# Pooled attention and two MLPs: keys by head into other rooms, looks behind attention, and the second MLP's tiles prepared one tile earlier

## The chip, the cores and the metric

One Trainium2 chip, one of its cores. The metric is the device time of one execution in microseconds (us). The kernel before takes 1679.4 us (median of three runs, 1678.56 to 1681.44).

## The reference

```python
k_p = k.reshape(B, H, Sp, pool, D).mean(axis=3)
v_p = v.reshape(B, H, Sp, pool, D).mean(axis=3)
scores = scale * np.matmul(q, k_p.transpose(0, 1, 3, 2))
scores = scores - np.max(scores, axis=-1, keepdims=True)
attn = np.exp(scores)
attn = attn / (np.sum(attn, axis=-1, keepdims=True) + 1e-09)
x = np.matmul(attn, v_p)
...
h = x @ w_in
g = np.where(h >= 1, h, np.where(h <= -1, 0.0, (h + 1) ** 2 / 4))
y = g @ w_out
...
h = y @ w2_in
g = h * (1.0 / (1.0 + np.exp(-h)))
return (g @ w2_out).astype(np.float32)
```

There are 8 batches of 8 heads, 576 positions and 64 features; keys and values are averaged over groups of 8 positions, so 72 remain of each. The result, 4608 tokens of 512 features, goes through two MLPs with 2048 hidden features. The weights come in 64 bits, and are read as pairs of 32-bit words.

## The kernel before, in words

**Precision.** A matrix product is made of three half-precision products: each operand is split into a high and a low half (`split`: ScalarE writes the high one, L354, VectorE the low one, L355), and L120, L121 and L122 multiply high by high, low by high and high by low. A "look" finds the largest absolute value of a tile, from which its power-of-two scale is made; a small TensorE product into a tile named `all` (L107, or L247 for the first weight) carries that maximum to all partitions.

**Stages.** (1) Attention for the first four tiles of 128 tokens, in single precision: keys and values of batch 0 are loaded by pairs of heads (L397 `kv_load`, four rooms of the pool `kvp` named `raw`); the keys are summed over groups of 8 on VectorE (L420), the values on TensorE by products with a unit matrix (L413). Then come transposes of the queries (L496), scores (L526), softmax on VectorE and ScalarE (L535 to L559, L540), transposes of the weights (L574), the product with the values (L614), and the split into `xh` and `xl` (L621). (2) The first weight, 8 MB, in nine pieces `wa_128` to `wa_136`: `load1`, `look1` (ScalarE L239 takes absolute values, VectorE L240 the maximum), `scales1` (L247, L250), and `convert1`, which assembles a 32-bit word on VectorE (L95 shift, L259, L262), scales and rounds it on ScalarE (L265, L267) and takes the low half on GpSimd (L268). (3) The first MLP: nine tiles of 512 tokens, each of 16 chunks; a chunk is a group of products `hps` (`emit_h`), the activation (`pre_A`, `min_A`, `mid_A`, `post_A`, with the split at L819 and L820), and, three chunks later (`LAG`), its share of the products `y` (`emit_yA`). `evac_yA` (L839) scales a finished tile into a room of the pool `big`, which has one room, and stores it to DRAM. The rest of the attention and the conversion of the other three weights run between the chunks. (4) The second MLP: 18 tiles of 256 tokens. `tile_B(t)` (L859) prepares one in six steps: load into the room of `big` (`yin`, L865), look (L111, then `all` L107), sums on GpSimd, and three splits. `group_B(t, q, ys)` (L893) makes the hidden features in two halves, q = 0 and 1; each has seven products `hb` of 24 matmuls (a scheme with seven instead of eight products), and between these it takes the seven output products `y` of the half before it out of the list `ys` (12 matmuls each). `evac_yB` (L977, adds at L986) reads the seven finished `y` banks of a tile into the rooms `ob` and stores them; it stands after the first half of the next tile.

**What sets the order.** The Python code is the program order of a scheduler that simulates the engines and lets an instruction that is ready go ahead of one that isn't; `paced` ties work to the time at which a named step (`late[...]`) is done. Rooms are reused when their last reader has finished.

**What the main loops say.** The second MLP asks for the next tile's first three steps ahead of the first half and for its splits ahead of the second:

```python
for t in range(NTB):
    for q in range(2):
        if t + 1 < NTB:
            if q == 0:
                pend.extend(tile_B(t + 1))
            for _ in range(3):
                pend.pop(0)()
        ys = group_B(t, q, ys)
        if q == 0 and t:
            evac_yB(t - 1)
```

Of the kernel before, what the change touches and what calls it, by code (L numbers as in the profile page):

```python
# [9 lines left out]
F32 = mybir.dt.float32  # L10
# [23 lines left out]
def tile_pooled_attention_two_mlps(  # L34
# [22 lines left out]
    POOL = 8  # L57
# [295 lines left out]
    def split(hi, lo, x, s):  # L353
        a = nc.scalar.activation(out=hi, in_=x, func=AF.Copy, scale=s)  # L354
        return a, nc.vector.scalar_tensor_tensor(out=lo, in0=x, scalar=s, in1=hi, op0=ALU.mult, op1=ALU.subtract)  # L355
# [37 lines left out]

    def kv_load(b, which, hp):

        r = kv_raw[b, which, hp] = kvp.tile([SP, 2, POOL, D], F32, tag="raw", name="raw")
        src = (k if which == "k" else v)[b, 2 * hp:2 * hp + 2]  # L397
        nc.sync.dma_start(out=r, in_=src.rearrange("h (p r) d -> p h r d", r=POOL))

    def kv_pool(b, which, hp):  # L400

        if hp == 0:
            sums[b, which] = kvp.tile([SPT, H, D], F32, tag="sum", name="sum", bufs=3)
            if which == "k":
                nc.gpsimd.memset(sums[b, which][SP // 32 * 32:SPT], 0.0)
        dst = sums[b, which][0:SP, 2 * hp:2 * hp + 2]
        r = kv_raw.pop((b, which, hp))
        if (b, which) in ON_PE:
            if hp == 0:
                kv_ps[b, which] = att_ps([SP, H, D])  # L410
            ps = kv_ps[b, which]
            for n in range(POOL):
                nc.tensor.matmul(  # L413
                    out=ps[:, 2 * hp:2 * hp + 2], lhsT=ident[0:SP, 0:SP], rhs=r[:, :, n], start=n == 0,
                    stop=n == POOL - 1,
                )
            if hp == NP - 1:
                nc.scalar.copy(out=sums[b, which][0:SP], in_=kv_ps.pop((b, which)))
        else:
            nc.vector.tensor_reduce(out=dst, in_=r.rearrange("p h r d -> p h d r"), axis=AX.X, op=ALU.add)  # L420
# [62 lines left out]
    q_t, qT_t, cq_t, at_t, aT_t, kT = {}, {}, {}, {}, {}, {}  # L483

    def load_q(i):
        q_t[i] = qp.tile([128, H, D], F32, tag="q", name="qt")
        for o, n, b, s in segs(i):
            nc.sync.dma_start(out=q_t[i][o:o + n], in_=q[b, :, s:s + n, :].rearrange("h p d -> p h d"))

# [109 lines left out]
    def att_pv(i):  # L599
# [21 lines left out]
        hi, lo = (x[:, :, j * 128:(j + 1) * 128] for x in r["x"])  # L621
        for o, n, b, _ in segs(i):
            c = b - t * N // S
            split(hi[:, :, o:o + n], lo[:, :, o:o + n], ps[:, :, o:o + n], r["sv"][:, c:c + 1])
        if j == 0 and t:
            consts_A(r)

# [211 lines left out]
    def evac_yA(t):  # L839
        r = XT.pop(t)  # L840
        cy = sm.tile([128, KD], F32, tag="cy", name="cy")
        ts(cy, e2, r["ge"], 2.0 ** -29, ALU.mult, ALU.mult)
        y = big.tile([128, KD, N], F32, tag="big", name="y32")
        for d, ps in enumerate(acc_t.pop(t)):
            if d % 2:
                ts(y[:, d], ps, cy[:, d:d + 1])
            else:
                nc.scalar.activation(out=y[:, d], in_=ps, func=AF.Copy, scale=cy[:, d:d + 1])
            nc.sync.dma_start(out=ydram[t][:, d], in_=y[:, d])


    TB = 256
# [4 lines left out]
    def tile_B(t):  # L857
# [18 lines left out]
        def sums_():  # L876
            b = held["b"]
            comb_b([held["z"][:, n] for n in range(4)], b[:, 0, 0], b[:, 0, 1], b[:, 1, 0], b[:, 1, 1])
            r["x"] = [x.rearrange("p c n -> p (c n)")[:, 0:7 * 256].rearrange("p (n c f) -> p n c f", n=7, c=2)
                      for x in new_x()]  # L880

        def part(a, b, x):
            hi, lo = (y[:, a:b] if b > a + 1 else y[:, a] for y in r["x"])
            split(hi, lo, x(), r["s"])

# [3 lines left out]
    def group_B(t, q, ys):  # L889
# [36 lines left out]
        add(c11, u, product(1, 1))  # L926
        act(c11)
        halves_of(0, c11)
        y(1)
        add(u, u, product(2, 5))  # L930
        y(1)
        add(v, u, product(3, 6))
# [21 lines left out]
        minus(z4, c21, z2)  # L954
        halves_of(1, c21)
        halves_of(2, z4)
        y(1)
        if q == 0:
            r["acc"] = [ps_y.tile([128, 2, 256], F32, tag=f"y{k_}", name=f"y{k_}") for k_ in range(4)]

# [97 lines left out]

    load_to(4)
    q_to(3)  # L1060
    load1(0)
    load_to(8)
    q_to(4)
    for p in range(1, len(cuts1)):
        load1(p)
    load_to(12)
    pool_to(4)
# [9 lines left out]
    r = XT[0]  # L1077
    for a, b in ((0, 3), (3, 7), (7, 9)):
        for p in range(a, b):
            look1(p)  # L1080
        scales1(a, b)
        if a == 0:
            convert1(0)
# [16 lines left out]
    for s in range(KF + 2):  # L1100
        if s < KF:
            while n1 < min(len(cuts1), piece_of(cuts1, s) + 2):
                convert1(n1)
                n1 += 1
            emit_h(s, chunk1, r["x"])
        z = s - 1
# [44 lines left out]
    for s in range(KF, LAST + LAG):  # L1151
# [30 lines left out]
                nc.sync.dma_start(out=w4[i], in_=d4[:, i])  # L1182
        if T == NTILE - 1 and m == 3:
            pend.extend(tile_B(0))
        if pend:
            pend.pop(0)()
        z = s - LAG
# [3 lines left out]
                evac_yA(z // KF)  # L1191

    wctx.close()
    b2 = bctx.enter_context(tc.tile_pool(name="b2", bufs=1, side="right", reuse_waits="tile"))
    for i in range(4, PIECES):
        w4.append(b2.tile([128, 2, 7, 256], F16, name=f"wd{i}"))
# [3 lines left out]
    ys = []  # L1200
    for t in range(NTB):
        for q in range(2):
            if t + 1 < NTB:
                if q == 0:
                    pend.extend(tile_B(t + 1))
                for _ in range(3):
                    pend.pop(0)()
            ys = group_B(t, q, ys)
            if q == 0 and t:
                evac_yB(t - 1)  # L1210
    for f in ys:
        f()
    evac_yB(NTB - 1)
# [31 lines left out]
```

## Time and profile before

| | |
|---|---|
| median of three runs | 1679.4 us (1678.56 to 1681.44) |
| the profiled execution, its own time | 1683.29 us |
| its span | 1681.4 us |
| mean granted TensorE clock | 0.965 of full speed |
| DMA traffic | 166.35 MB, mean 99 GB/s |
| TensorE busy | 93% of the span |
| VectorE busy | 75% of the span |
| ScalarE busy | 53% of the span |
| GpSimd busy | 32% of the span |

The span runs from the first to the last recorded instruction; 1.9 us of the execution's own time lie around it. A row of the timeline gives start, duration, engine, line, operation, and behind it in brackets how long the engine had been idle and what ended that. Lines are those of the kernel before unless it is said otherwise; in the changed kernel L413 is L426, L614 is L630, L820 is L836, L910 is L934, L986 is L1010, and L239 to L355 stay.

### The profile page before, as it was taken

To read this page: it belongs to the slowest core of one execution; us is meant where nothing else is said; L and a number is where in the kernel's file an instruction comes from. 1 tells how busy PE (TensorE), PEld (TensorE's weight loads), DVE (VectorE), ACT (ScalarE), POOL (GpSimd) and SP (SyncE) were. 2 spreads that over 40 slices of the span, in tenths; PEclk is the share of its full clock that TensorE was granted. 3 is DMA by queue.
4 is the path that set the end of the run, shared out by engine and by line. 5 is a ranking of instruction groups with operands and counts; after the bars stand their busy time and mean duration, and the time that the engine had idled before them with its cause. 6 is when DMAs were issued, how large, how long until landed. Compare 5 with 4: busy or idle time off the path is not lost.

```text
span 1681.4 us, 34695 instructions
## 1 busy us (share of the span) xinstructions
PE 1561.3 (93%) x14406; PEld 1078.8 (64%) x14406; DVE 1255.0 (75%) x2204; ACT 894.9 (53%) x1420; POOL 534.7 (32%) x479
## 2 busy tenths in 40 slices
PE   6894799898999999999999979999999999999998
PEld 6542344344444444444444459999999999999998
DVE  7798887978889787897656338777766777777765
ACT  3577354666747547576655435455444454444543
POOL 1322402332424303333422023443333343334322
PEclk7897899899999999999999989999999999999999
DMA  9435587655646576353454030000100001000000
GB/s 278 129 99 140 140 218 174 145 129 137 166 118 161 141 218 167 98 131 86 133 220 148 0 138 27 27 27 27 37 30 27 27 27 39 27 27 27 27 14 27
DMA packets 217037, 166.35 MB, mean 99 GB/s; under 512 B 153904, under 2 KB 176432, under 8 KB 216880
## 3 DMA queue, kind: packets, MB, share of 16 engines
q1 hardware_dynamic: 216880, 164.14, 35.1%
q8 instruction: 113, 1.85, 0.5%
q14 instruction: 44, 0.36, 0.1%
HBM read 102.76 MB, written 33.55 MB: 81 GB/s over the span
## 4 chain that ended last, share of the span: by engine, by line
PE 31%; DVE 26%; issue 15%; ACT 10%; DMA 8%; POOL 8%; SPq 1%; DVEq 0%; POOLq 0%; ACTq 0%
DMA yin<-y 4%; PE y L120 4%; PE y L122 4%; PE y L121 4%; POOL c L681 4%; DVE sum L420 4%; DVE g L355 4%; PE hps L122 4%; PE hps L121 4%; PE hps L120 4%; DVE g L791 3%; POOL c L684 2%; DVE xl L355 2%; DVE g L820 2%; ACT g L354 2%
## 5 line engine op out<-in xcount | busy, mean ns | idle before, releaser
L121 PE MATMUL hb<-xl,wc 128*128 128x128 f16 x2016 | 349.7, 219 | 0.0
L120 PE MATMUL hb<-xh,wc 128*128 128x128 f16 x2016 | 349.7, 219 | 0.0
L122 PE MATMUL hb<-xh,wc 128*128 128x128 f16 x2016 | 349.7, 219 | 0.0
L355 DVE SCALAR_TENSOR_TENSOR g<-c,tsg,g 128x512 f16<-128x512 f32 x252 | 226.6, 902 | 87.8 <-ACT g L354 87.8
L973 PE MATMUL y<-wd,g 128*128 128x256 f16 x1008 | 274.7, 273 | 14.4 <-DVE ob L986 13.0
L975 PE MATMUL y<-wd,g 128*128 128x256 f16 x1008 | 274.8, 273 | 1.0 <-DVE g L355 0.9
L974 PE MATMUL y<-wd,g 128*128 128x256 f16 x1008 | 274.7, 273 | 0.0
L913 ACT ACTIVATE c<-c,tc 128x512 f32<-128x512 f32 x144 | 103.0, 717 | 258.8 <-DVE c L910 258.8
L120 PE MATMUL y<-g,wb 128*128 128x512 f16 x544 | 207.7, 388 | 17.3 <-ACT wb L212 15.0
L120 PE MATMUL hps<-xh,wa 128*128 128x512 f16 x576 | 221.0, 384 | 1.3 <-ACT g L780 0.9
L354 ACT ACTIVATE g<-c,tsg 128x512 f16<-128x512 f32 x252 | 177.6, 718 | 83.7 <-POOL c L684 51.3
L121 PE MATMUL hps<-xl,wa 128*128 128x512 f16 x576 | 220.9, 383 | 0.3 <-DVE skv L95 0.3
L122 PE MATMUL hps<-xh,wa 128*128 128x512 f16 x576 | 220.6, 384 | 0.0
L910 DVE TENSOR_TENSOR c<-c,hb 128x512 f32<-128x512 f32 x252 | 167.7, 680 | 70.4 <-PE hb L122 70.1
L121 PE MATMUL y<-g,wb 128*128 128x512 f16 x544 | 211.2, 388 | 5.8 <-DVE g L820 5.8
L122 PE MATMUL y<-g,wb 128*128 128x512 f16 x544 | 210.5, 387 | 4.1 <-POOL wb L213 3.9
L121 PEld LDWEIGHTS <-wc 128*128 128x128 f16 x2016 | 197.7, 98 | 2.6
L120 PEld LDWEIGHTS <-wc 128*128 128x128 f16 x2016 | 197.7, 98 | 2.1
L122 PEld LDWEIGHTS <-wc 128*128 128x128 f16 x2016 | 197.7, 98 | 0.2
L791 DVE SCALAR_TENSOR_TENSOR g<-g,tbr,u 128x512 f32<-128x512 f32 x144 | 127.4, 886 | 59.2 <-ACT u L787 58.0
L681 POOL TENSOR_TENSOR c<-c 128x512 f32<-128x512 f32 x108 | 163.8, 1530 | 2.8
L787 ACT ACTIVATE u<-u,trsg 128x512 f32<-128x512 f32 x144 | 103.3, 719 | 103.8 <-DVE u L93 103.8
(179 smaller groups left out, 2719.7 us busy)
## 6 DMA issues: line engine op xcount, KB each, us to landing
raw<-in_moe_w_out_dram SPq DMA_DIRECT2D x24, 1024.0 KB
raw<-in_moe_w_in_dram SPq DMA_DIRECT2D x18, 1024.0 KB
raw<-in_k_dram SPq DMA_DIRECT2D x32, 288.0 KB
raw<-in_v_dram SPq DMA_DIRECT2D x32, 288.0 KB
y<-y SPq DMA_DIRECT2D x36, 256.0 KB
yin<-y SPq DMA_DIRECT2D x18, 512.0 KB
out_dram<-ob SPq DMA_DIRECT2D x36, 256.0 KB
qt<-in_q_dram SPq DMA_DIRECT2D x32, 256.0 KB
```

The costliest lines, as they stand in the source:

```text
L120: nc.tensor.matmul(out=acc, lhsT=wh, rhs=xh, start=start, stop=False)
L121: nc.tensor.matmul(out=acc, lhsT=wh, rhs=xl, start=False, stop=False)
L122: nc.tensor.matmul(out=acc, lhsT=wl, rhs=xh, start=False, stop=stop)
L354: a = nc.scalar.activation(out=hi, in_=x, func=AF.Copy, scale=s)
L355: return a, nc.vector.scalar_tensor_tensor(out=lo, in0=x, scalar=s, in1=hi, op0=ALU.mult, op1=ALU.subtract)
L681: nc.gpsimd.tensor_tensor(out=out, in0=a, in1=b, op=ALU.subtract)
L787: nc.scalar.activation(out=u_t[s], in_=u_t[s], func=AF.Square, scale=r["rsg"])
L791: return nc.vector.scalar_tensor_tensor(out=g32_t[s], in0=g32_t[s], scalar=r["br"], in1=u_t.pop(s), op0=ALU.subtract, op1=ALU.max)
L910: nc.vector.tensor_tensor(out=out, in0=x, in1=y, op=ALU.add)
L973: nc.tensor.matmul(out=acc, lhsT=xh, rhs=wh, start=start, stop=False)
L974: nc.tensor.matmul(out=acc, lhsT=xh, rhs=wl, start=False, stop=False)
L975: nc.tensor.matmul(out=acc, lhsT=xl, rhs=wh, start=False, stop=stop)
```

## The change

It has four parts.

*Early loads.* Batch 0's keys are loaded and summed by single heads: eight loads and eight sums of 64 columns instead of four of 128, into rooms `g` of the pool `gp`, which the first MLP fills only later. That leaves the four `raw` rooms to the values, whose loads now follow the first three query loads. The fourth query tile goes into a room `u` of the pool `up`. All of these loads stand ahead of the first piece of the first weight.

*Looks behind attention.* The looks from the fourth piece on, and the conversions from the third (`n1` = 1) on, are paced by the last split of the attention (`late["x"]`).

*The second MLP's tiles prepared earlier.* The last `evac_yA` writes into four rooms of `up` instead of the room of `big`. `tile_B(1)`'s load, look and sums are asked for within the last tile of the first MLP and its splits at the start of the second; after that, tile t + 2 is loaded at the end of tile t, its look and sums stand ahead of the first half of tile t + 1, and its splits ahead of that tile's second half. The rooms for the splits are taken at the first split (`room()`).

*Output products in the second half.* With q = 1 the first place takes none (`y(1 - q)`) and the last takes two (`y(1 + q)`). So three products `hb` (72 matmuls) stand ahead of the first `y` of that half, where two (48) stood before.

```diff
--- before.py
+++ after.py
@@ -393,6 +393,12 @@
 
     def kv_load(b, which, hp):
 
+        if (b, which) == (0, "k"):
+            for h in (2 * hp, 2 * hp + 1):
+                r = gp.tile([128, 2, N], F16, tag="g", name="k0").rearrange("p a n -> p (a n)").bitcast(F32)
+                r = kv_raw[b, which, h] = r[0:SP].rearrange("p (r d) -> p r d", r=POOL)
+                nc.sync.dma_start(out=r, in_=k[0, h].rearrange("(p r) d -> p r d", r=POOL))
+            return
         r = kv_raw[b, which, hp] = kvp.tile([SP, 2, POOL, D], F32, tag="raw", name="raw")
         src = (k if which == "k" else v)[b, 2 * hp:2 * hp + 2]
         nc.sync.dma_start(out=r, in_=src.rearrange("h (p r) d -> p h r d", r=POOL))
@@ -404,6 +410,13 @@
             if which == "k":
                 nc.gpsimd.memset(sums[b, which][SP // 32 * 32:SPT], 0.0)
         dst = sums[b, which][0:SP, 2 * hp:2 * hp + 2]
+        if (b, which) == (0, "k"):
+            for h in (2 * hp, 2 * hp + 1):
+                nc.vector.tensor_reduce(
+                    out=sums[b, which][0:SP, h], in_=kv_raw.pop((b, which, h)).rearrange("p r d -> p d r"),
+                    axis=AX.X, op=ALU.add,
+                )
+            return
         r = kv_raw.pop((b, which, hp))
         if (b, which) in ON_PE:
             if hp == 0:
@@ -483,7 +496,10 @@
     q_t, qT_t, cq_t, at_t, aT_t, kT = {}, {}, {}, {}, {}, {}
 
     def load_q(i):
-        q_t[i] = qp.tile([128, H, D], F32, tag="q", name="qt")
+        if i == NI - 1:
+            q_t[i] = up.tile([128, N], F32, tag="u", name="q3").rearrange("p (h d) -> p h d", h=H)
+        else:
+            q_t[i] = qp.tile([128, H, D], F32, tag="q", name="qt")
         for o, n, b, s in segs(i):
             nc.sync.dma_start(out=q_t[i][o:o + n], in_=q[b, :, s:s + n, :].rearrange("h p d -> p h d"))
 
@@ -621,7 +637,7 @@
         hi, lo = (x[:, :, j * 128:(j + 1) * 128] for x in r["x"])
         for o, n, b, _ in segs(i):
             c = b - t * N // S
-            split(hi[:, :, o:o + n], lo[:, :, o:o + n], ps[:, :, o:o + n], r["sv"][:, c:c + 1])
+            late["x"] = split(hi[:, :, o:o + n], lo[:, :, o:o + n], ps[:, :, o:o + n], r["sv"][:, c:c + 1])[1]
         if j == 0 and t:
             consts_A(r)
 
@@ -840,13 +856,17 @@
         r = XT.pop(t)
         cy = sm.tile([128, KD], F32, tag="cy", name="cy")
         ts(cy, e2, r["ge"], 2.0 ** -29, ALU.mult, ALU.mult)
-        y = big.tile([128, KD, N], F32, tag="big", name="y32")
+        if t < NTILE - 1:
+            y = big.tile([128, KD, N], F32, tag="big", name="y32")
+            ys = [y[:, d] for d in range(KD)]
+        else:
+            ys = [up.tile([128, N], F32, tag="gu"[d % 2], name="y32") for d in range(KD)]
         for d, ps in enumerate(acc_t.pop(t)):
             if d % 2:
-                ts(y[:, d], ps, cy[:, d:d + 1])
+                ts(ys[d], ps, cy[:, d:d + 1])
             else:
-                nc.scalar.activation(out=y[:, d], in_=ps, func=AF.Copy, scale=cy[:, d:d + 1])
-            nc.sync.dma_start(out=ydram[t][:, d], in_=y[:, d])
+                nc.scalar.activation(out=ys[d], in_=ps, func=AF.Copy, scale=cy[:, d:d + 1])
+            nc.sync.dma_start(out=ydram[t][:, d], in_=ys[d])
 
 
     TB = 256
@@ -876,10 +896,14 @@
         def sums_():
             b = held["b"]
             comb_b([held["z"][:, n] for n in range(4)], b[:, 0, 0], b[:, 0, 1], b[:, 1, 0], b[:, 1, 1])
+
+        def room():
             r["x"] = [x.rearrange("p c n -> p (c n)")[:, 0:7 * 256].rearrange("p (n c f) -> p n c f", n=7, c=2)
                       for x in new_x()]
 
         def part(a, b, x):
+            if a == 0:
+                room()
             hi, lo = (y[:, a:b] if b > a + 1 else y[:, a] for y in r["x"])
             split(hi, lo, x(), r["s"])
 
@@ -926,7 +950,7 @@
         add(c11, u, product(1, 1))
         act(c11)
         halves_of(0, c11)
-        y(1)
+        y(1 - q)
         add(u, u, product(2, 5))
         y(1)
         add(v, u, product(3, 6))
@@ -954,7 +978,7 @@
         minus(z4, c21, z2)
         halves_of(1, c21)
         halves_of(2, z4)
-        y(1)
+        y(1 + q)
         if q == 0:
             r["acc"] = [ps_y.tile([128, 2, 256], F32, tag=f"y{k_}", name=f"y{k_}") for k_ in range(4)]
 
@@ -1058,10 +1082,9 @@
 
     load_to(4)
     q_to(3)
-    load1(0)
     load_to(8)
     q_to(4)
-    for p in range(1, len(cuts1)):
+    for p in range(len(cuts1)):
         load1(p)
     load_to(12)
     pool_to(4)
@@ -1077,7 +1100,10 @@
     r = XT[0]
     for a, b in ((0, 3), (3, 7), (7, 9)):
         for p in range(a, b):
-            look1(p)
+            if a:
+                paced(lambda: look1(p), "x")
+            else:
+                look1(p)
         scales1(a, b)
         if a == 0:
             convert1(0)
@@ -1100,7 +1126,7 @@
     for s in range(KF + 2):
         if s < KF:
             while n1 < min(len(cuts1), piece_of(cuts1, s) + 2):
-                convert1(n1)
+                paced(lambda: convert1(n1), "x")
                 n1 += 1
             emit_h(s, chunk1, r["x"])
         z = s - 1
@@ -1182,6 +1208,9 @@
                 nc.sync.dma_start(out=w4[i], in_=d4[:, i])
         if T == NTILE - 1 and m == 3:
             pend.extend(tile_B(0))
+            rest = tile_B(1)
+            pend.extend(rest[:3])
+            rest = rest[3:]
         if pend:
             pend.pop(0)()
         z = s - LAG
@@ -1191,6 +1220,7 @@
                 evac_yA(z // KF)
 
     wctx.close()
+    pend = rest
     b2 = bctx.enter_context(tc.tile_pool(name="b2", bufs=1, side="right", reuse_waits="tile"))
     for i in range(4, PIECES):
         w4.append(b2.tile([128, 2, 7, 256], F16, name=f"wd{i}"))
@@ -1200,14 +1230,14 @@
     ys = []
     for t in range(NTB):
         for q in range(2):
-            if t + 1 < NTB:
-                if q == 0:
-                    pend.extend(tile_B(t + 1))
-                for _ in range(3):
-                    pend.pop(0)()
+            for _ in range(min(len(pend), 3 if q else 2 if t else 0)):
+                pend.pop(0)()
             ys = group_B(t, q, ys)
             if q == 0 and t:
                 evac_yB(t - 1)
+        if t + 2 < NTB:
+            pend = tile_B(t + 2)
+            pend.pop(0)()
     for f in ys:
         f()
     evac_yB(NTB - 1)
```

**VectorE, from the last values of the first attention to the scales of the first weight, before.** `xl` are the low halves of attention's splits, `cols` the maxima and scales of the weight's pieces.

```order
L355 SCALAR_TENSOR_TENSOR v_114<-sum,skv,v_114 72x512
L559 RECIPROCAL den<-den 128x8
L240 TENSOR_SCALAR wa_136,cols<-wa_136 128x1024
L556 TENSOR_SCALAR den<-den 128x8
L355 SCALAR_TENSOR_TENSOR xl<-att,tsv,xh 128x4x128
L355 SCALAR_TENSOR_TENSOR xl<-early,tsv,xh 128x4x128
L559 RECIPROCAL den<-den 128x8
L355 SCALAR_TENSOR_TENSOR xl<-att,tsv,xh 128x4x128
L250 TENSOR_REDUCE cols<-all 128x3
L93 TENSOR_SCALAR cols<-cols 128x3
L95 TENSOR_SCALAR cols<-cols 128x3 x2
L355 SCALAR_TENSOR_TENSOR xl<-att,tsv,xh 128x4x128
```

Of the nine looks one, at piece 136, stands in this piece, ahead of the splits, and the other eight stand above it.

The same place in the changed kernel:

```order
L355 SCALAR_TENSOR_TENSOR v_114<-sum,skv,v_114 72x512
L355 SCALAR_TENSOR_TENSOR xl<-att,tsv,xh 128x4x128
L355 SCALAR_TENSOR_TENSOR xl<-early,tsv,xh 128x4x128
L355 SCALAR_TENSOR_TENSOR xl<-att,tsv,xh 128x4x128 x2
L240 TENSOR_SCALAR wa_131,cols<-wa_131 128x512
L240 TENSOR_SCALAR wa_132,cols<-wa_132 128x512
L240 TENSOR_SCALAR wa_133,cols<-wa_133 128x1024
L240 TENSOR_SCALAR wa_134,cols<-wa_134 128x1024
L240 TENSOR_SCALAR wa_135,cols<-wa_135 128x1024
L95 TENSOR_SCALAR xf<-wa_129 128x1024
L95 TENSOR_SCALAR xf<-wa_130 128x1024
L240 TENSOR_SCALAR wa_136,cols<-wa_136 128x1024
```

The looks at pieces 131 to 136 stand behind the last of the four splits and ahead of the scales; before, only the scales (L250) were left there.

**VectorE, from the last chunk of the first MLP to the first tile of the second, before.** `g` are activations, `y` the tile that `evac_yA` writes, `m` the maximum of a tile `yin`, `c` a product of the second MLP.

```order
L820 TENSOR_TENSOR g_9687<-g_9666,g_9687 128x512
L93 TENSOR_SCALAR y_9716<-y_9220,cy 128x512
L93 TENSOR_SCALAR y_9716<-y_9222,cy 128x512
L910 TENSOR_TENSOR c<-c,hb 128x512
L355 SCALAR_TENSOR_TENSOR g_9829<-c,tsg,g_9829 128x512
L111 TENSOR_REDUCE m_9751<-yin 128x1
L108 TENSOR_REDUCE te<-all 128x1
L93 TENSOR_SCALAR te<-te 128x1 x2
```

The look at tile 1 (L111) stands here behind the evacuation (L93) and behind an add of the second MLP.

The same place in the changed kernel:

```order
L93 TENSOR_SCALAR u<-g_9700,tlim 128x512
L355 SCALAR_TENSOR_TENSOR xl<-yin,ts,xh 128x512
L355 SCALAR_TENSOR_TENSOR xl<-yin,ts,xh 128x256
L355 SCALAR_TENSOR_TENSOR xl<-yin,ts,xh 128x1024
L807 SCALAR_TENSOR_TENSOR g_9700<-g_9700,tbr,u 128x512
L836 TENSOR_TENSOR g_9721<-g_9700,g_9721 128x512
L111 TENSOR_REDUCE m_10324<-yin 128x1
L93 TENSOR_SCALAR y_9751<-y_9237,cy 128x512
L93 TENSOR_SCALAR y_9753<-y_9239,cy 128x512
L934 TENSOR_TENSOR c<-c,hb 128x512 x2
L355 SCALAR_TENSOR_TENSOR g_9842<-c,tsg,g_9842 128x512
```

Tile 1's splits (`xl<-yin`) now stand in front of the last chunk's activation, and the look at tile 2 (L111) in front of the first MLP's last evacuation (L93), where before the look at tile 1 came behind both and behind the second MLP's first adds.

## Rows read from the trace of the kernel before

**Rows 1.** The page, part 1: busy us of each engine (share of the span) xinstructions.
```profile
PE 1561.3 (93%) x14406; PEld 1078.8 (64%) x14406; DVE 1255.0 (75%) x2204; ACT 894.9 (53%) x1420; POOL 534.7 (32%) x479
```

**Rows 2.** Windows, 980 to 1000: span, busy PE PEld DVE ACT POOL, PEclk, DMA share, GB/s.
```profile
980.00:990.00 10.00, 0.17 (x1) 0.17 (x2) 1.22 (x1) 0.00 (x0) 1.22 (x2) 0.65 0.73 293
990.00:1000.00 10.00, 10.00 (x146) 9.84 (x147) 8.41 (x18) 4.83 (x7) 2.59 (x5) 0.84 0.17 54
```

**Rows 3.** Who waited for whom, TensorE, 970 to 1100: us, times, longest.
```profile
PE all L107 <- DVE m L111: 10.2, 1, 10.2
PE y L973 <- DVE ob L986: 2.2, 3, 1.5
PE y L973 <- ACT g L354: 1.3, 3, 0.7
PE y L975 <- DVE g L355: 0.9, 2, 0.6
```

**Rows 4.** Timeline, 965 to 990: start us, us, what [idle before].
```profile
965.80 0.69 DVE L820 TENSOR_TENSOR g<-g,g 128x512 f16<-128x512 f32 x1 [0.68 <-ACT g L819]
...
969.79 1.03 PE L120 MATMUL y<-g,wb 128*128 128x512 f16 x4
...
978.64 0.55 SPq L865 DMA_DIRECT2D yin<-y  x1
...
988.56 1.22 DVE L111 TENSOR_REDUCE m<-yin 128x1 f32<-128x1024 f32 x1 [10.25 <-DMA yin<-y]
...
989.83 0.80 PE L107 MATMUL all<-ident,m 128*128 128x128 f32 x2 [10.20 <-DVE m L111]
```

**Rows 5.** Who waited for whom, TensorE, 1100 to 1600.
```profile
PE y L973 <- DVE ob L986: 10.8, 14, 1.5
```

**Rows 6.** Timeline, one tile of the second MLP, where TensorE waits in it.
```profile
1153.21 0.27 PE L973 MATMUL y<-wd,g 128*128 128x256 f16 x1
...
1156.15 0.86 DVE L986 SCALAR_TENSOR_TENSOR ob<-y,cyb,ub 128x256 f32<-128x256 f32 x2
...
1156.68 0.27 PE L973 MATMUL y<-wd,g 128*128 128x256 f16 x1 [0.60 <-DVE ob L986]
...
1156.94 0.67 DVE L910 TENSOR_TENSOR c<-c,hb 128x512 f32<-128x512 f32 x1
```

**Rows 7.** Windows, the 38.08 us of that tile, columns as in rows 2.
```profile
1139.53:1177.61 38.08, 37.48 (x510) 35.46 (x508) 27.83 (x48) 18.39 (x28) 14.39 (x12) 1.00 0.09 29
```

**Rows 8.** Timeline, start to the first converted weight.
```profile
16.07 1.97 PE L526 MATMUL early<-k,qT 128*128 128x144 f32 x8
...
31.79 7.03 PE L413 MATMUL early<-raw,ident 72*72 72x128 f32 x32
...
46.49 1.10 ACT L239 ACTIVATE wa<-wb 128x1024 f32<-128x1024 f32 x1
...
59.48 3.21 ACT L265 ACTIVATE xf<-xf,cols 128x1024 f32<-128x1024 f32 x3
...
59.62 0.75 DVE L355 SCALAR_TENSOR_TENSOR xl<-att,tsv,xh 128x512 f16<-128x512 f32 x1 [0.29 <-ACT xh L354]
...
61.02 4.81 PE L413 MATMUL att<-raw,ident 72*72 72x128 f32 x42
...
65.87 2.33 DVE L95 TENSOR_SCALAR xf<-wa 128x512 int32<-128x512 int32 x1 [2.38 <-POOL wa L268]
```

**Rows 9.** Lines by form, 0 to 66: what it is xcount | busy us, mean ns | idle before.
```profile
L413 PE MATMUL early<-raw,ident 72*72 72x128 f32 x64 | 14.2, 420 | 5.1 <-DMA raw<-in_v_dram 5.1
...
L240 DVE TENSOR_SCALAR_CACHE_REDUCE wa<-wa 128x1024 f32<-128x1024 f32 x7 | 8.4, 1206 | 2.0 <-ACT wa L239 2.0
...
L95 DVE TENSOR_SCALAR xf<-wa 128x1024 int32<-128x1024 int32 x3 | 2.7, 903 | 0.0
...
L262 DVE SCALAR_TENSOR_TENSOR xf<-raw,xf 128x1024 int32<-128x1024 int32 x2 | 2.4, 1192 | 0.0
```

**Rows 10.** Windows, 28 to 32, columns as in rows 2.
```profile
28.00:32.00 4.00, 4.00 (x20) 3.76 (x19) 4.00 (x9) 1.25 (x2) 1.14 (x1) 0.50 1.10 248
```

## The prediction, made before any run of the changed kernel

> **What bounds the kernel now.** First the page's busy times: TensorE is busy 93% of the span, VectorE 75% [rows 1]. The kernel ends when TensorE's matmuls end, so what can be won is TensorE's idle time and the time it runs at its lower clock. Three places have such time, and the change touches all three. (a) The seam of the two MLPs: the view of waits shows one stop of 10.2 us, on the `all` of the look at tile 1, and 1.3 and 0.9 us on freshly split activations [rows 3]; the windows show TensorE 0.17 us busy in the 10 us from 980, and a mean granted clock of 0.65 in these and 0.84 in the next 10, in which it is busy throughout [rows 2]. (b) The second MLP: 2.2 us in three waits up to 1100 [rows 3] and 10.8 us in 14 up to 1600 [rows 5], all of a `y` product for the adds of `evac_yB`: 13.0 us in 17 of 18 tiles. (c) The start: the first converted weight is out on GpSimd when VectorE goes on at 65.87 us [rows 8]; from there conversions on VectorE set the pace, and nothing makes up for a later start.
>
> **(a) The seam.** The tile's load is issued at 978.64, because the one room of `big` has to be emptied first, and lands 10 us later: VectorE had been idle for 10.25 us when it began the look at 988.56; TensorE's `all` followed at 989.83 [rows 4]. After the change `evac_yA(8)` no longer uses that room, and tile 1's look and sums are finished inside the first MLP. Gone: 10.2 us; the 1.3 and 0.9 us that follow while TensorE catches up with fresh splits; and of the next 10 us the part lost to the clock, 10 × (1 − 0.84) = 1.6 us. Together 14.0 us. Bounds: 14.2, with the 0.17 us that TensorE worked at the lower clock before 990 [rows 2], and 9, if only the long wait goes and 1.2 us of it (one look, 1.22 us [rows 4]) comes back elsewhere. What is late next: tile 1's splits now stand on VectorE ahead of the last chunk's activation, three of them, which by the split of 0.69 us [rows 4] and the sizes (512, 256 and 1024 columns) take some 2.5 us. Before, the last chunk's split ended at 966.49 and its products began at 969.79 [rows 4]: 3.3 us of slack cover them; without that cover TensorE would wait up to 2.5 us. The look at tile 2 (1.22 us) stands ahead of the last evacuation; its load has the whole tile to land, now that 3.7 MB of second weights (four pieces of 128 × 3584 half-precision numbers) are what it competes with. I take 14.0, the row's own waits.
>
> **(b) The steady waits.** In one tile the first `y` of the second half starts at 1153.21; the second one, due when one product `hb` has passed, starts only at 1156.68, after 0.60 us of waiting for an add that began at 1156.15 [rows 6]. It shares its bank with output parts that this add reads last. A tile takes 38.08 us, TensorE 37.48 us of it busy [rows 7]; it has 28 equal steps (14 products `hb`, 14 `y`), so one step takes (38.08 − 0.6) / 28 = 1.34 us. With three products instead of two ahead of the first `y`, the second `y` is due 1.34 us later, at 1156.08 + 1.34 = 1157.4, and the bank is free at 1156.68: 0.7 us to spare. No work is added; the `y` left out returns at the end of the half. I take 12.4 of the 13.0 us as gained, since the longest waits were 1.5 us [rows 3, 5], 0.2 us more than a step. Bounds: all 13.0, or 4, when two thirds of every wait return in a later place. What is late next is the third product's bank: VectorE's add of the second product starts at 1156.94 and takes 0.67 us [rows 6]; product six, which needs that bank, starts six steps behind the first `y`'s old start, at 1153.21 + 6 × 1.34 = 1161.2, so there are 3.6 us to spare.
>
> **(c) The start.** Loads of keys, queries and values ahead of the first weight let the values be summed at once. TensorE's scores ended at 16.07 + 1.97 = 18.04 [rows 8]; one group of four of them now stands behind, which leaves 17.3. The sums of the values are 64 records and take 14.2 us [rows 9], at half clock: 32 of them took 7.03 us at 31.79, and 42 later ones 4.81 us [rows 8], and in the window from 28 TensorE is busy 4.00 of 4 us at a granted clock of 0.50 [rows 10]. So they end at 31.5 where they ended at 38.82 before (31.79 + 7.03). From there the last split ended 21.5 us later, at 60.37 (59.62 + 0.75 [rows 8]); I take 20, since ScalarE has as many looks between these steps as before, VectorE fewer. Last split: 51.5. But now six looks follow on VectorE, two of half width, 5 × 1.21 = 6.0 us; four assemblies of 1.19 make 4.8, two shifts of 0.90 make 1.8 [rows 9]; some 1.5 us of small scales (an estimate from the rows' order); together 14. From there to the first converted weight 6.4 us, as before between 59.48 and 65.87 [rows 8]. Sum 51.5 + 14 + 6.4 = 71.9 against 65.87: **6 us lost**. Bounds: gain of 3.4, if the looks are done as the weight lands (the last ScalarE look began at 46.49 and took 1.10 [rows 8]; then a VectorE look 1.2, the assemblies and scales 7.3, and 6.4: 62.5); loss of 10, if the 21.5 us and a further 2.5 us of ScalarE's looks in the way return.
>
> **At nothing:** eight loads of keys for four (the issues hide behind the transfers, which are as many bytes; without cover each costs one issue, 0.55 us [rows 4], 2.2 in all); 30 pooling matmuls of the next batch's keys ahead of the first `hps`, 60 records at the two paces of 0.11 and 0.22 us 7 to 13 us, beside the 14 + 6.4 us of looks and assemblies (without cover, as much as that); keys in rooms `g`, empty until the first MLP's activations; the order of stores and loads on SP's queue, idle there.
>
> **Sum.** −14.0 − 12.4 + 6 = −20.4. The profiled execution took 1683.29 us, 3.9 above the median 1679.4; so it becomes 1662.9, and **1659** on the basis of the median.
>
> **The rivals.**
> *The clock rises during the values' sums.* All four pairs of values arrive together, TensorE has no stop for loads between them as before, and the sums could run at the pace of the later ones: 64 × 4.81 / 42 = 7.3 us instead of 14.2 [rows 8, 9]. Then the start loses nothing, but gains 1: **1652**. For it: the later records ran at full speed. Against it: TensorE was busy without a stop at 0.50 [rows 10]. The Trainium skill, "TensorE: Matmul & The Clock Gate", section "Part 1: The HAM clock gate", says that the default state is throttled and activity releases it; by that rule this rival is the likelier one. The trace does not agree here, with 4.00 of 4 us busy at 0.50.
> *The waits of (b) only move.* The third `y` finds its bank still read by the adds, which all come in one row on VectorE, and waits some 0.5 us in each of 17 tiles: 8 of 12.4 us come back: **1667**. Against it: VectorE is busy 27.83 of 38.08 us [rows 7].
> *The seam only moves.* The look at tile 2 stands ahead of the evacuation on VectorE, in program order; if its load lands late among the second weights (10 us as before [rows 4]), the evacuation waits, TensorE's `y` banks stay full, and the 10 us stand one step ahead: **1669**. Against it: that load is asked for a tile earlier.
> *Slower.* Three products back to back in the second half need banks faster than VectorE empties them. If the second product's add comes later than now by more than its 3.6 us, TensorE waits for the excess in each of 18 tiles. The gain of 20.4 is used up at 1.13 us a tile, that is a delay of 4.7 us; at 5.6 it is 2.0 × 18 = 36 us: **1695**. Against it: in the tile read the add comes right behind the adds of `evac_yB`, and nothing new stands before it.
> *It does not do what it says.* Another room or queue (SP's, behind stores) keeps tile 1 and the waits where they are: about **1679**.
>
> **How the numbers follow.** Forecast 0.55, clock rival 0.24, moved waits 0.08, moved seam 0.08, slower 0.03, no effect 0.02. The forecast's own bounds, with its terms not all at their ends at once, are 1652 to 1665. The range 1646 to 1669 takes in the forecast, the clock rival with the upper bound of the start, and most of the moved waits and seam; it leaves out the slower case, no effect and the ends, under 2 in 10. Some 0.2%, or 3.4 us, is what a measurement can tell from no change (three runs spread over 2.9 us). Faster by more than that: all cases but the last two, with a little off, 0.96; the same 0.01; slower 0.03.
>
> **What would show it.** In the seam no wait of `all` near 975 to 990 and a clock of 1.0 there. In the second MLP no waits of `y` for `ob` in the second half, a tile of 37.4 us, and no new wait of `hb` on L934. At the start VectorE's restart at 72 rather than 66 us, the last `xl` near 51.5, and the granted clock during the sums of values: 0.50 for the forecast, 1.0 for the first rival. I am wrong if TensorE waits elsewhere in the second MLP for over 5 us, if the last chunk's activation waits for tile 1's splits, or if VectorE's restart lies below 64 or above 76 us.

## The result, and the profile after

The changed kernel takes **1653.3 us** (median of four runs, 1651.41 to 1654.58) against 1680.35 us for the kernel before in the same series: ratio 0.9839, 95% interval 0.9822 to 0.9856, so 27.0 us less (24 to 30). The forecast was 1659, the range 1646 to 1669. Profiled executions compare 1683.29 with 1653.36 us, 29.9 less.

Where it came from is read at four marks that both traces have, as the start of the same instruction in each (timelines of ScalarE and of the DMA issues):

| mark | before | after | after − before | change since the mark above |
|---|---|---|---|---|
| first store of the first MLP's first tile | 214.86 | 219.01 | +4.2 | +4.2 |
| last scaling of its last tile | 972.15 | 973.76 | +1.6 | −2.5 |
| first output copy of the second MLP | 1037.03 | 1021.48 | −15.6 | −17.2 |
| last one | 1674.50 | 1644.86 | −29.6 | −14.1 |

So the seam gave 17, the second MLP's tiles 14, and the start lost 4, of which 2.5 came back in the middle of the first MLP. That stretch, between the first and the second mark, takes from 752.8 to 757.8 us in the thirteen traces, so 2.5 us is no more than executions differ by; the 4 us at the start hang on the execution, too, as is shown below. The page of the changed kernel, part 1, as in [rows 1]:

```profile
PE 1557.4 (94%) x14406; PEld 1077.8 (65%) x14406; DVE 1262.8 (76%) x2208; ACT 895.2 (54%) x1420; POOL 536.5 (32%) x479
```

TensorE's busy time is nearly what it was, 1557.4 for 1561.3 us; what went is the rest of the span, 94.2 (1651.6 − 1557.4) for 120.1 us (1681.4 − 1561.3).

**Seam.** The windows of the changed kernel, as in [rows 2], and one tile of its second MLP (from the first output copy of one tile to that of the next), as in [rows 7]:

```profile
980.00:990.00 10.00, 10.00 (x167) 9.82 (x165) 7.53 (x9) 6.57 (x10) 5.78 (x4) 1.00 0.77 309
990.00:1000.00 10.00, 10.00 (x129) 9.38 (x128) 6.76 (x11) 4.36 (x7) 2.05 (x2) 1.00 0.01 2
1321.18:1358.27 37.09, 36.66 (x496) 34.63 (x494) 28.00 (x48) 18.50 (x30) 14.40 (x13) 1.00 0.09 30
```

TensorE is busy all through at clock 1.00; before it was busy 0.17 and 10.00 at 0.65 and 0.84. The view of waits has no row for TensorE between 970 and 1100 (four before [rows 3]), and one between 1100 and 1600, where 10.8 us stood [rows 5]:

```profile
PE y L997 <- DVE ob L1010: 0.4, 1, 0.4
```

VectorE's timeline around the last chunk shows why nothing was pushed ahead of the seam:

```profile
964.75 1.15 DVE L355 SCALAR_TENSOR_TENSOR xl<-yin,ts,xh 128x512 f16<-128x512 f32 x2
...
966.19 1.28 DVE L355 SCALAR_TENSOR_TENSOR xl<-yin,ts,xh 128x1024 f16<-128x1024 f32 x1 [0.29 <-ACT xh L354]
...
968.82 0.69 DVE L836 TENSOR_TENSOR g<-g,g 128x512 f16<-128x512 f32 x1 [0.68 <-ACT g L835]
...
971.39 1.22 DVE L111 TENSOR_REDUCE m<-yin 128x1 f32<-128x1024 f32 x1 [1.88 <-DMA yin<-y]
...
973.27 1.61 DVE L93 TENSOR_SCALAR y<-y,cy 128x512 f32<-128x512 f32 x2 [0.66 <-PE y L122]
```

Tile 1's splits take 2.4 us (1.15 + 1.28) at 964.75 and 966.19, in front of the activation, whose last step ends at 969.51 instead of 966.49 [rows 4]; 1 us of these 3 was there already in the chunk before (this step starts at 961.67 instead of 960.62). TensorE does not stop: the first products `hb` of the second MLP go in between (one starts at 970.84). The look at tile 2 waits 1.88 us for its load; the evacuation behind it starts at 973.27 instead of 971.72, and by then it waits for TensorE's last `y` product (0.66 us), not for the look. No wait of TensorE follows.

**Start.** The changed kernel's timelines of TensorE, VectorE and ScalarE, as in [rows 8], and two windows, as in [rows 10]:

```profile
17.39 7.37 PE L426 MATMUL early<-raw,ident 72*72 72x128 f32 x64
...
51.91 1.23 PE L247 MATMUL all<-ident,cols 128*128 128x128 f32 x4 [3.16 <-DVE cols L250]
52.93 13.01 PE L426 MATMUL att<-raw,ident 72*72 72x128 f32 x60
...
65.73 0.63 PE L120 MATMUL hps<-xh,wa 128*128 128x512 f16 x1
```

```profile
42.79 1.62 DVE L355 SCALAR_TENSOR_TENSOR xl<-att,tsv,xh 128x512 f16<-128x512 f32 x2 [4.33 <-ACT xh L354]
...
44.33 0.68 DVE L240 TENSOR_SCALAR_CACHE_REDUCE wa<-wa 128x512 f32<-128x512 f32 x1
...
59.35 0.14 DVE L93 TENSOR_SCALAR tlim<-tsg 128x1 f32<-128x1 f32 x1
...
63.97 2.33 DVE L95 TENSOR_SCALAR xf<-wa 128x512 int32<-128x512 int32 x1 [4.48 <-POOL wa L268]
```

```profile
57.58 3.23 ACT L265 ACTIVATE xf<-xf,cols 128x1024 f32<-128x1024 f32 x3 [12.93 <-DVE cols L95]
```

```profile
20.00:24.00 4.00, 4.00 (x39) 4.00 (x38) 1.89 (x5) 1.15 (x1) 2.77 (x3) 1.00 1.05 386
...
52.00:56.00 4.00, 4.00 (x19) 4.00 (x20) 4.00 (x7) 0.00 (x0) 0.00 (x0) 0.50 0.10 31
```

The 64 records of the values take 7.37 us, not 14.2 [rows 9], at clock 1.00: the first rival's case. The last split ends at 44.41 (42.79 + 1.62), 16 us sooner than before; then come the six looks and the assemblies up to 59.49, and VectorE goes on at 63.97, 1.9 us sooner [rows 8]. Yet the first `hps` starts at 65.73: TensorE is held by 60 records of the next batch's sums. They stand behind the `all` products of the first weight, which wait for the looks and scales on VectorE, so they start only at 52.93; and they run at clock 0.50 and take 13.01 us. TensorE had been busy for only 0.75 and 0.09 us of the two stretches of 2 us from 48 and 50, at that clock already.

What then turned 1.9 us of gain into 4.2 of loss stands on ScalarE and TensorE. ScalarE of the changed kernel and of the kernel before, then TensorE of the one and of the other:

```profile
109.90 1.12 ACT L174 ACTIVATE xf<-raw 128x1024 f32<-128x1024 f32 x1 [3.63 <-DMA raw<-in_moe_w_out_dram]
...
112.11 0.57 ACT L431 COPY sum<-att 72x512 f32<-72x512 f32 x1
```

```profile
109.08 0.56 ACT L418 COPY sum<-att 72x512 f32<-72x512 f32 x1
...
112.68 1.15 ACT L174 ACTIVATE xf<-raw 128x1024 f32<-128x1024 f32 x1
```

```profile
113.35 0.80 PE L107 MATMUL all<-ident,cols 128*128 128x128 f32 x2 [6.13 <-ACT rows L438]
...
141.43 1.17 PE L537 MATMUL att<-kT,qT 128*64 128x72 f16 x32 [9.71 <-DMA qT<-rows]
...
143.38 0.77 PE L107 MATMUL all<-ident,wm 128*128 128x128 f32 x2 [0.78 <-DVE sq L95]
...
150.71 0.61 PE L120 MATMUL y<-g,wb 128*128 128x512 f16 x1 [6.56 <-ACT wb L212]
```

```profile
109.22 0.49 PE L107 MATMUL all<-ident,cols 128*128 128x128 f32 x2 [1.24 <-ACT rows L425]
...
132.94 1.17 PE L521 MATMUL att<-kT,qT 128*64 128x72 f16 x32 [6.68 <-DMA qT<-rows]
...
136.08 0.77 PE L107 MATMUL all<-ident,wm 128*128 128x128 f32 x2 [1.96 <-DVE e L536]
...
146.18 0.61 PE L120 MATMUL y<-g,wb 128*128 128x512 f16 x1 [9.33 <-ACT wb L212]
```

On ScalarE, L174 (absolute values of the second weight's third piece) stands ahead of L431, the copy of value sums of batch 1; before, the copy (L418) came first. Its data, issued at 102.60, let ScalarE wait 3.63 us. The sums come late, TensorE stands 6.13 us at the `all` behind them, the next scores, which wait for the transposes of the queries, start 8.5 us later (141.43 against 132.94), the `all` of the second weight (143.38 against 136.08) stands in TensorE's queue behind these scores, and the first `y` starts at 150.71 instead of 146.18.

These times are those of one execution each, and the start of one and the same code differs. With the loads and looks of the kernel before, the first `y` starts at 146.18 (kernel before), 147.63 (run of the preparation alone), 142.41 (of the second half's products alone) and 141.92 us (of all but the early part); with the early part it starts at 150.71, 150.09 (the changed kernel again) and 149.22 us (early part alone). So it is later in each pair, by 1.6 to 8.8 us and by 5.5 in the mean, and the 4.2 of the table is one pair. The value sums are where the four differ; the last section has their times.

### The profile page after: what moved, and what is told of

It reads as the page before. It is cut to its first block, busy times and chain, and to the rows that moved or that the text cites. A ratio compares the mean times of both kernels' runs of the same rounds, so it can differ in the third digit from the quotient of the medians.

```text
span 1651.6 us, 34720 instructions
## 1 busy us (share of the span) xinstructions
PE 1557.4 (94%) x14406; PEld 1077.8 (65%) x14406; DVE 1262.8 (76%) x2208; ACT 895.2 (54%) x1420; POOL 536.5 (32%) x479
## 4 chain that ended last, share of the span: by engine, by line
PE 43%; DVE 25%; issue 10%; ACT 9%; POOL 6%; DMA 6%; SPq 0%; DVEq 0%; POOLq 0%; ACTq 0%
DVE sum L433 4%; PE y L120 4%; PE y L997 4%; PE y L122 4%; POOL c L697 4%; PE y L999 4%; PE y L121 4%; PE y L998 4%; PE hb L121 3%; PE hb L120 3%; PE hb L122 3%; PE hps L122 3%; PE hps L121 3%; PE hps L120 3%; DVE g L807 3%
```

## The experiments

In the diffs, lines marked + are what the run has. A gain in us is worked out from the ratio; where the medians give another, it stands beside it. The runs were made in three series, each with the kernel before beside them (medians 1678.42, 1678.71 and 1677.58); times of different series are compared by their ratios.

### The parts one by one

**Second half's products alone.** Against the kernel before:

```diff
-        y(1)
+        y(1 - q)
...
-        y(1)
+        y(1 + q)
```

> Only the output products' places in the second half are changed (72 instead of 48 matmuls ahead of the first y). Theory: the waits of y for the ob adds go by themselves, 12 to 13 us of 13.0; about 1667 us, a tile of 37.4 us, the 10.2 us wait at the seam as before. Rival: the waits go only because the next tile is prepared a tile earlier, too, which takes VectorE steps out of the adds' way; then over half of the 13 us is still there, 1673 us or more. A third point: in the kernel before, TensorE's weight loads of the y products also stopped for some 6 us between 1200 and 1400 with no releaser shown (issue); if these hang on the order of the products they are gone here, if they hang on the execution they may be here or not.

Measured: ratio 0.991 (0.9887 to 0.9934), 15.1 us less; median 1664.8 of five executions, 13.6 less. A sixth, of which the profile was taken, took 4743.75 us, for a reason that is not known, and is left out; so the same kernel was profiled again:

> The second half's output products alone once more, for its profile. Theory: the y waits for the ob adds, 13.0 us in 17 tiles before, are under 1 us, the tile takes 37.1 us as in the change, and the stop of about 10 us at the seam is there as before. Rival (the tile's preparation has a part in it): over 4 us of y waits left, a tile of 37.5 us or more.

Its time was 1663.99. Who waited for whom, TensorE, 970 to 1100 and 1100 to 1600:

```profile
PE all L107 <- DVE m L111: 10.6, 1, 10.6
...
PE y L973 <- DVE ob L986: 0.6, 1, 0.6
...
PE y L973 <- DVE ob L986: 2.5, 4, 1.1
```

Of 13.0 us 3.1 are left, more than the 1 expected and less than the rival's 4: five waits, four of them between 1222 and 1337 us, where the tiles are long in every run (last section). Outside of that stretch a tile takes some 37.1 us, and the wait at the seam is untouched. With the preparation as well, 0.4 and 1.7 us are left in the two traces of the changed kernel and 1.9 in that of all but the early part, so the preparation has a small part in it at most.

**Preparation alone.** Only the hunks on `evac_yA`, `tile_B` and the loops that call it:

> Only the second MLP's tiles are prepared earlier, with the last evacuation in rooms of the pool up. Theory: the seam's wait goes with its lower clock, 14 to 17 us, and the y waits for ob stay at about 13 us; 1663 to 1666 us. Rival: the earlier look also shortens the y waits; 1660 us or less with under 7 us of them left. Second rival: the wait at the seam comes back a step ahead, under 6 us gained, 1674 us or more.

Measured: 1663.73, ratio 0.9909 (0.9889 to 0.9928), 15.3 us less (14.7 by the medians). The waits of TensorE, 1100 to 1600:

```profile
PE y L981 <- DVE ob L994: 10.9, 13, 1.5
```

They stay as they were; the second half's waits don't hang on the preparation.

**Early part alone.** The hunks on loads, rooms and pacing:

> Only the early part: keys by head in other rooms, loads ahead of the first weight, looks and conversions paced behind attention; seam and second MLP as before. Theory from the two traces: VectorE goes on with the first weight at 64 us, 1.9 us sooner, but the first tile's y products start late behind the second weight's first piece, so that the tile's store is 4 us later and 1 to 2 us are left at the end of the first MLP: 1681 to 1684 us. Rival (what is gained at 64 us lasts): 1678 to 1679 us.

Measured: 1685.43, ratio 1.0032 (1.0017 to 1.0047): 5.4 us slower (7.0 by the medians), more than expected.

**All but the early part.**

> The whole change without its early part. Theory: the two parts add up, 28 to 31 us; 1650 to 1652 us, 1 to 2 us under the changed kernel, whose early part loses that much. Rival (the early part gains 2 us): 1655 us or more.

Measured: 1648.72, ratio 0.9818 (0.9797 to 0.9840), 30.6 us less; 15.1 + 15.3 = 30.4, so the two add up (by the medians 29.7 and 28.3).

### What in the early part costs

**Loads without pacing, and pacing without loads.** The first has the change with these lines as before:

```diff
-            if a:
-                paced(lambda: look1(p), "x")
-            else:
-                look1(p)
+            look1(p)
...
-                paced(lambda: convert1(n1), "x")
+                convert1(n1)
```

> The change without its pacing: early loads, seam and second half as in the change, but looks and conversions not held behind attention. Theory: the loads are good and the pacing is the loss. The looks are done as the weight lands, beside attention, VectorE goes on with the first weight some 6 us sooner than the changed kernel's 63.97, at 57 to 59 us, and the second weight's third look stands behind the copy of the value sums again, so that the first y products start at 146 us or earlier (150.7 in the changed kernel); 1645 to 1649 us. Rival: the loads, which hold the first weight back, are the loss; no better than the changed kernel, 1653 us or more.

> The change without its early loads: looks and conversions held behind attention, loads in the order of the kernel before. Theory: the attention ends at about 60 us as in the kernel before and 6 looks and the assemblies come behind it on VectorE, so that VectorE goes on with the first weight at 70 us or later; slower than seam and second half alone (1648.7) by 4 to 9 us: 1653 to 1658. Rival (the start is made up for before the first y products): 1649.

Measured: 1646.91, ratio 0.981 (0.9793 to 0.9827), without the pacing; 1656.45, ratio 0.9868 (0.9854 to 0.9883), without the loads. In the first, VectorE goes on at 61.00 (57 to 59 was expected) and the first `y` starts at 142.47; in the second, VectorE goes on at 75.31. Against the kernel with neither (ratio 0.9818), the loads are worth some 1 us, within the intervals, and the pacing costs some 8 us. With the loads the pacing costs 4.9 us by the ratios (0.9839 and 0.981), and 5.1 side by side in one series (below). So it is the pacing that loses; and without it the early part is not shown to be better than none.

**ScalarE's third look put back.** The changed kernel with two lines more:

```diff
-                nc.scalar.copy(out=sums[b, which][0:SP], in_=kv_ps.pop((b, which)))
+                late["sum"] = nc.scalar.copy(out=sums[b, which][0:SP], in_=kv_ps.pop((b, which)))
...
-            run(*work2[d + 1])
+            paced(work2[d + 1][0], "sum")
+            run(*work2[d + 1][1:])
```

> The changed kernel with one step more: the second weight's third piece may have its absolute values taken on ScalarE only behind the copy of the sums of the values. Theory: the loss of 4 us at the first y products comes from that step, which in the changed kernel stands ahead of the copy in ScalarE's queue and waits 3.6 us for a load issued only at 102.6; the stop of 6.1 us at the all near 113 goes to under 2 us, the first y products start at about 146 to 147 us instead of 150.7; 1648 to 1650 us. Rival: attention's transposes are late for another reason; the first y products stay at 150 us, 1653 us.

Measured: 1649.40, ratio 0.9828 (0.9815 to 0.9842). By the medians that is 3.9 us under the changed kernel, by the ratios 1.8, with intervals that overlap; the time alone does not show the step. TensorE of this run:

```profile
110.31 0.49 PE L107 MATMUL all<-ident,cols 128*128 128x128 f32 x2 [2.94 <-ACT rows L438]
...
134.30 1.17 PE L537 MATMUL att<-kT,qT 128*64 128x72 f16 x32 [7.34 <-DMA qT<-rows]
...
146.06 0.61 PE L120 MATMUL y<-g,wb 128*128 128x512 f16 x1 [6.19 <-ACT wb L212]
```

The stop at the `all` is 2.94 us (under 2 was expected), the first `y` starts at 146.06. In the three traces with the whole early part and without these two lines the look stands ahead of the copy, waits 3.63, 3.30 and 3.14 us for its load, and the first `y` starts at 150.71, 150.09 and 149.22. So the order on ScalarE is worth 3 to 5 us at the first `y`. It is not all that the pacing costs: without the pacing, in the same series, the first `y` starts at 142.47, and the time is 2.5 us shorter (1646.91, all runs of it under all of this one).

**The better version, beside the change.** Both on one chip:

> The changed kernel itself, on the same chip as the next run. Expected 1651 to 1655 us, as before.

> The change without its pacing once more, beside the changed kernel. Theory (the pacing costs): 4 to 8 us under it, 1645 to 1649 us. Rival (the chips differ, not the kernels): within 2 us of it.

Measured: 1652.46 (1650.37 to 1654.33) and 1647.34 (1646.34 to 1649.71), 5.1 us apart, and no run of the one lies among those of the other. The change without its pacing beats both kernels.

### The clock in the sums of the values

Two runs with the loads of the change without its pacing, and one, then three, pieces of the first weight between the values. The diff is that of three pieces, against the changed kernel; the lines of the pacing are as above:

```diff
     load_to(4)
     q_to(3)
+    load_to(6)
+    load1(0)
+    load1(1)
+    load1(2)
     load_to(8)
     q_to(4)
-    for p in range(len(cuts1)):
+    for p in range(3, len(cuts1)):
```

> As the change without its pacing, with one load moved: the first piece of the first weight, 1 MB, stands between the first two and the last two loads of values, as a stop in TensorE's sums of the values. Theory: it is a stop of some us of TensorE there that lets the granted clock fall, as in the kernel before (2.2 and 2.9 us); the sums take 11 to 14 us at a clock of 0.50 in place of 7.4, and 1 to 6 us are lost against the run without the move. Rival: the clock falls or not from one execution to the next, whatever the loads; sums at 7 to 8 us and no loss.

> As the run with one load moved, which made no stop, but with three pieces (3 MB) of the first weight between the first two and the last two loads of values, so that TensorE must stop for some 3 to 6 us in the middle of the sums. Theory: the stop lets the granted clock fall to 0.50; the second half of the sums takes 6 to 7 us instead of 3.7. Rival: the clock does not care for a stop; 3.7 us again for the second half.

One piece made no stop (two runs of 32 records, 3.66 us each, 0.3 us apart), so that run tells nothing of a stop: 1648.04, against 1646.91 without the move, within the intervals. Three pieces did. TensorE's timeline and windows of that run:

```profile
16.18 3.66 PE L426 MATMUL early<-raw,ident 72*72 72x128 f32 x32
...
20.58 1.07 PE L590 MATMUL att<-ident,e 128*72 128x128 f32 x8 [0.25 <-POOL e L576]
...
23.05 0.60 PE L590 MATMUL early<-ident,e 128*72 128x128 f32 x4 [1.41 <-POOL sum L411]
...
25.77 7.10 PE L426 MATMUL early<-raw,ident 72*72 72x128 f32 x32 [2.11 <-DMA raw<-in_v_dram]
```

```profile
16.00:20.00 4.00, 4.00 (x38) 4.00 (x37) 3.87 (x10) 2.35 (x4) 0.63 (x1) 1.00 1.05 388
20.00:24.00 4.00, 2.00 (x15) 1.28 (x13) 4.00 (x8) 2.42 (x4) 2.62 (x3) 1.00 1.06 309
28.00:32.00 4.00, 4.00 (x20) 4.00 (x19) 4.00 (x8) 1.38 (x2) 0.00 (x0) 0.50 1.04 346
```

The same 32 records take 3.66 us ahead of the stops (1.41 and 2.11 us, with TensorE busy 2.00 of 4 us from 20 to 24) and 7.10 us behind, at 0.50. So one kind of work runs at either level here, and the fall came with the stops. The Trainium skill describes the like ("TensorE: Matmul & The Clock Gate", section "HAM oscillation — how this bites in real kernels"): in a kernel whose steps wait for a transfer, the wait throttles TensorE again and the next step starts slow. The trace agrees: 3.66 against 7.10 us. What lifts the clock again isn't shown by these runs. Later in the same run it stayed at 0.50 for 28 us in which TensorE was busy nearly throughout:

```profile
44.00:72.00 28.00, 27.74 (x131) 21.77 (x129) 20.24 (x38) 13.94 (x18) 10.03 (x6) 0.50 0.54 149
```

The 3.4 us that the second half of the sums lost are not to be seen in the time: 1648.85, ratio 0.9829 (0.9804 to 0.9854), against 1647.34 without the move in the same series, 1.5 us more and within the intervals.

## Why the prediction was right, and where its steps were not

- **(a) Seam, −14.0:** right in mechanism, and in size within what was measured: 15.3 alone, 12 to 19 by the interval. TensorE's idle time before, 970 to 1010, is 12.5 us by the windows, and the clock cost 1.6; the marks give 17.2. Of the 3 us between, some 1.3 us (an estimate) are the tails described in the last section, in about eight stops; some 2 us stay open. One of the prediction's signs of being wrong came true and cost nothing: the last chunk's activation did wait for tile 1's splits, but the slack of 3.3 us held.
- **(b) Steady waits, −12.4:** right in place and cause, and in size within what was measured: 15.1 alone, 11 to 19 by the interval, and 14.1 by the marks. A tile took 38.08 us and takes 37.09, a little less than the 37.4 forecast: the step "13.0 us of waits" counted what the view shows, and a stop costs more. (The 17 waits stand in 15 tiles, not 17; two tiles have two.) The slack for the second product held: no new wait of `hb` is in the trace.
- **(c) Start, +6:** the net came out (5.4 alone; 3.5 and 5.5 within the change, by the ratios of its two series against 0.9818), but by luck: two errors of opposite sign cancelled. The step that failed is "at half clock" for the sums of the values: I took the clock of the trace before for a property of this work. The sums took 7.37 us and ended at 24.76, not 31.5. The steps behind them were sized well: "20" was 19.7, "14" behind the last split 13.2 (44.41 to 57.58), "6.4" was 6.4 (57.58 to 63.97). So VectorE went on at 63.97, not 71.9, which is just below the 64 that the prediction gave as a sign of being wrong. The first rival had that, and its 1652 is the nearest number; but its gain of 1 us was not what the start gave. What lost time in place of the sums: the 30 pooling matmuls that I put at nothing, "beside the 14 + 6.4 us", started only at 52.93, took 13.01 us and held the first `hps` until 65.73, where VectorE had been released by the first converted weight at 63.97; and that the new order on ScalarE would move a look ahead of the sums, 3 to 5 us at the first `y`, I had not seen.
- **The number:** the forecast for the profiled execution was 1662.9, and the one measured took 1653.36, 9.5 less. The marks put 3.2 of that on the seam, 1.7 on the tiles, and 4.4 on the start up to the second mark, where 1.6 us were lost and not 6. By the medians the forecast was 5.7 too high.
- The other rivals: of the moved y waits 0.4 us is left, 1.7 in a second trace (8 were its price), the seam did not move ahead, and neither the slower case nor no effect came.

## What to carry to other kernels

Stops of an engine that are there for different reasons add up when taken away one by one, and each part is worth a run of its own: here two parts won 30 us and hid a third that lost 5. An order that holds work back behind a milestone moves everything else in the queues, too; look at what now stands ahead of it, above all an instruction whose load is issued late. A clock read from a trace belongs to the stops of that trace, and to that execution: read the same stretch in a second one before a term is built on it.

## What the runs showed of the hardware

A stop costs TensorE more than the idle time that the view of waits gives. At the wait of [rows 6] the last `hb` starts at 1155.86 and the `y` behind it at 1156.68, 0.82 us, where 0.06 us lie between two `hb` without a wait; the view says 0.60, because the record of the last matmul goes on for 0.22 us in which the next would have been issued. The loss is 0.76 us, 0.16 more than shown; over 17 stops that is 2.7 us (an estimate from this one stop), of the size by which (b) was short, 1.7 by the marks.

The clock of the value sums also differed from one execution to the next of the same early code. With the loads and looks as before, the last 32 records took 7.03 us in the kernel before and in the run of the preparation alone, and 4.40 and 4.24 in the runs without the early part and of the second half's products alone, which are the two with the early first `y`. The two gaps ahead of them were 2.17 and 2.89, 2.97 and 4.14, 0.48 and 3.82, 0.81 and 4.30 us; but in the run of the pacing alone they were 0.75 and 2.56, and the records took 7.03. So the lengths of these gaps alone don't tell which it will be, and what does was not tried. With the loads of the change, where no gap is left, all 64 records took 7.15 to 7.37 us in each of six traces.

One point of the first expectation is left open: between 1150 and 1350 TensorE's weight loads of the `y` products stop with no releaser shown, 7.2, 6.7 and 7.4 us in the kernel before and in the runs of the preparation and of the early part, and 0.9, 2.1 and 3.0 us in the changed kernel, without its early part, and with the second half's products alone. They go with the order of the products, but the tiles of that stretch stay longer than the others in all of them (38.7 to 39.4 beside 38.0 in the kernel before, 37.5 to 37.9 beside 37.1 in the changed one), so what makes them long is not known.
